# A sliding-window attention with a two-layer network behind it: a batch's last 64-query block and the next batch's first block are scored together

## The chip, the cores and the metric

The kernel runs on one core of one Trainium2 chip. A core has a TensorE (PE in the profile) for matmuls, a VectorE (DVE), a ScalarE (ACT), a GpSimd (POOL) and a SyncE (SP); the last two are used here to issue DMAs, and GpSimd for one iota. PE reads its stationary operand with a separate weight load (PEld). The metric is the device time of one execution in microseconds; the figure that counts is the median of several runs.

## The reference

Attention over 8 batches of 8 heads, 576 positions and 64 features a head, with a linear position bias and a causal window of 128; then a network of two matmuls with a squared ReLU between them, over all 4608 tokens.

```python
scores = np.matmul(q, k.transpose(0, 1, 3, 2)) / sqrt(64)
rel = pos[:, None] - pos[None, :]
mask = (rel >= 0) & (rel < 128)
scores = np.where(mask, scores - slopes[h] * abs(rel), -1e9)   # slopes[h] = 2 ** -(h + 1), 8 heads
attn = softmax(scores) @ v                                     # [8, 8, 576, 64]
x = attn.transpose(0, 2, 1, 3).reshape(4608, 512)
out = np.maximum(x @ w_in, 0) ** 2 @ w_out                     # w_in 512 x 2048, w_out 2048 x 512
```

## The kernel before

**Blocks.** A batch's 576 positions are cut into five blocks, four of 128 and a last one of 64 (`blk`); there are 40 blocks `m`, and `m % 5` is the place in the batch. As the window is 128 wide, a block's queries see the keys of their own block (part 1) and of the one before (part 0); the first block of a batch has part 1 alone. `attention(m)` (L294) does for one block:

- *turn*: K and Q of the block (tile `kq`, loaded by POOL at L276) are transposed into `kqT`. Blocks 0 to 9 do it by eight PE transposes into a PSUM tile `tp` (L317), copied out by DVE (L290) and ACT (L292); from block 10 on by one DMA transpose on SP's queue (`turn_kq`).
- *burst* (L347): the score matmuls of all eight heads, scores transposed (keys on partitions, queries on columns). A head has 64 features, so each matmul uses 64 of the 128 rows of the array, and two heads (`half` 0 and 1) follow each other on the two halves. A middle block has 16 of 128 columns; the last block of a batch 16 of 64 columns; the first block 8 of 128 columns. They go into four PSUM banks of tag `a`.
- *exp* (L360, ACT): four instructions, one a bank, of 512 elements a partition for a middle block and 256 for a last or first block, into a tile `P`.
- *mask* (L368, DVE): four multiplications of `P` by `masks`, which hold exp of the bias inside the window and 0 outside.
- *pv* (L383): P times V for each head and part, with a column of ones in V that sums the weights; then reciprocal (L404) and normalization (L409) on DVE for each half of the heads, into a tile `x`.
- *x turned*: into `xT`, by four PE transposes `xp` (L428) and a copy for blocks 0 to 12, by a DMA transpose on SP for later ones.

**The network.** Tokens go in nine groups of 512. `fc_step` (L461) makes one 128-wide slice of the hidden layer with four 128x512 matmuls into `h`, ACT takes the ReLU (L470), DVE the square (L476). `t_part` (L490) makes a quarter of the 16 matmuls of one 128-token output tile `o`, which ACT copies out (L501) and SP stores.

**Who sets the order.** Nothing is left to a scheduler on the chip: every step is a `Task` with an engine (or a choice of two), a key (its due time), what it depends on, and the `Slot`s of the rings it takes and gives back. `Plan.order()` plays the tasks through with assumed costs and gives each engine its list; the tasks are then emitted in that order, and each engine works through its list in order. So a change of the tasks rearranges all engines, POOL's loads and SP's queue too. The attention of later blocks is laid between the h and o matmuls of earlier groups. Group 0 needs blocks 0 to 3 of batch 0, group 1 blocks 4 to 8. Rings: four PSUM banks `a` (a burst takes all four), two each for `h` and `o`; four `kq`, four `kqT`, six `vt`, three `P`, three `x`.

Of the kernel before, what the change touches and what calls it, by code (L numbers as in the profile page):

```python
# [141 lines left out]
def kernel(  # L142
# [26 lines left out]

    ident = const.tile([128, 128], BF16)  # L170
    masks = const.tile([128, H, 2, 128], BF16)
    dist = const.tile([128, 2, 128], FP32)
    far = const.tile([128, 2, 128], FP32)
    w_in_sb = const.tile([128, C, d_ff], BF16)
# [5 lines left out]

    size = {"kq": 4, "v": 6, "kqT": 4, "P": 3, "x": 3}
    kq = ring("kq", size["kq"], [128, 2, d_model])
    vt = ring("vt", size["v"], [128, H, D + 1])
    kqT = ring("kqT", size["kqT"], [128, 2 * C, 128])
# [41 lines left out]
    for h in range(H):  # L228
        def build_mask(h=h):
            nc.scalar.activation(masks[:, place(h)], dist, AF.Exp, bias=0.0,  # L230
                                 scale=-(2.0 ** (-8.0 * (h + 1) / H)))
        t_mask.append(plan.add({"ACT": act(256)}, -9e5 + h, build_mask, [t_dist]))

    def ones():
        for t in vt:
# [55 lines left out]
        else:  # L291
            nc.scalar.activation(o, i, AF.Copy)  # L292

    def attention(m):  # L294
        b, kb = divmod(m, NKB)
        n = blk[kb]
        due = (b * S + kb * 128 + n) / 4 - 192 - 40
        first = b == 0
        kq_by_dma = m >= KQ_DMA
        x_by_dma = m >= X_DMA  # L300


        sk = sk_of[m] = Slot("kqT")
        both = {"ACT": act(C * n), "DVE": dve(C * n, 2)}
# [25 lines left out]
        t_kq_of[m] = t_kq  # L330


        sP = Slot("P")
        t_P = []
        parts = ([(0, m - 1)] if kb else []) + [(1, m)]
        p0 = parts[0][0]
        slot_s = [Slot("a") for _ in range(4)]

        def burst():

            for sl in slot_s:
                sl.tile = psum.tile([128, 512], FP32, tag="a", bufs=4, name="ps_s")
            for c in range(C):
                for part, mk in parts:
                    for half in range(2):
                        rows = slice(half * 64, half * 64 + 64)
                        nc.tensor.matmul(  # L347
                            slot_s[2 * (c // 2) + half].tile.rearrange("p (c t q) -> p c t q", c=2, t=2)[
                                :, c % 2, part, 0:n],
                            kqT[sk_of[mk].idx][rows, c, :], kqT[sk.idx][rows, C + c, 0:n], start=True, stop=True)  # L350
        rel = [sk_of[mk] for part, mk in parts if part == 0 or kb == NKB - 1]
        tm = plan.add({"PE": 220.0 + C * len(parts) * (max(n, 64) / 2.4 + 4)}, due - 28, burst,
                      [t for _, mk in parts for t in t_kq_of[mk]] + chain["s"], slot_s + [sP], rel)
        chain["s"] = [tm]
        for i in range(4):
            def view(t):
                return t[:, :, p0:2, 0:n]

            def expo(i=i):
                nc.scalar.activation(view(Pt[sP.idx][:, 2 * i:2 * i + 2]),  # L360
                                     view(slot_s[i].tile.rearrange("p (c t q) -> p c t q", c=2, t=2)),
                                     AF.Exp, bias=0.0, scale=scale)
            cols = 2 * n * len(parts)
            te = plan.add({"ACT": act(cols)}, due - 28 + 3 * i, expo, [tm], [], [slot_s[i]])

            def mask(i=i):
                pt = view(Pt[sP.idx][:, 2 * i:2 * i + 2])
                nc.vector.tensor_tensor(pt, pt, view(masks[:, 2 * i:2 * i + 2]), op=ALU.mult)  # L368
            t_P.append(plan.add({"DVE": dve(cols, 2)}, due - 28 + 3 * i, mask, [te] + t_mask))


        sx = Slot("x")
        t_norm = []
        for hf in range(2):
            slot_v = Slot("o" if first else "a")
            last = None
            for hi in range(4):
                h = 4 * hf + hi
                for part, mk in parts:
                    def emit(h=h, hi=hi, part=part, mk=mk, slot_v=slot_v):  # L380
                        if hi == 0 and part == p0:
                            slot_v.tile = psum.tile([128, 512], FP32, tag=slot_v.tag, bufs=plan.bufs[slot_v.tag], name="pv")
                        nc.tensor.matmul(  # L383
                            slot_v.tile[:, hi * (D + 1):(hi + 1) * (D + 1)],
                            Pt[sP.idx][:, place(h), part, :], vt[s_in[mk, "v"].idx][:, h, :],
                            start=part == p0, stop=part == 1)
                    rel = []
                    if hf == 1 and hi == 3:
                        if part == 0 or kb == NKB - 1:
                            rel.append(s_in[mk, "v"])  # L390
                        if part == 1:
                            rel.append(sP)
                    new = hi == 0 and part == p0
                    last = plan.add({"PE": mm(D + 1)}, due - 12 + 4 * hf, emit,
                                    [last, t_P[place(h) // 2], t_in[mk, "v"]]
                                    + (t_P[2 * hf:2 * hf + 2] + chain["pv"] if new else []),
                                    ([slot_v] + ([sx] if hf == 0 else [])) if new else [], rel)
# [37 lines left out]
                     slot_x.tile[:, 0:512].rearrange("p (c t) -> p c t", c=C)[:, :, 0:n])  # L435
            t_xT[b, kb] = plan.add(both if first else {"DVE": both["DVE"]}, due, evac, [last], [], [slot_x])

    sk_of, t_kq_of = {}, {}
    for m in range(NBLK):
        attention(m)  # L440


    def tokens(lo, hi):
# [116 lines left out]
```

The softmax here doesn't subtract the row's maximum and nothing guards it: scores larger than these inputs give would overflow.

## Time and profile before

| | |
|---|---|
| median of 5 runs | 321.72 us (321.22 to 323.79) |
| the profiled execution | 321.04 us |
| its span, first to last instruction | 319.3 us |
| PE busy | 304.2 us, 95% of the span, 2436 matmuls |
| DVE busy, ACT busy, POOL busy | 169.3 us, 178.5 us, 107.4 us |
| granted TensorE clock | 1.000 |
| chain that ended last, by engine | PE 92%, DVE 3%, the rest 1% or less each |

The page gives busy time as the union of an engine's instructions, and "idle before" as the time an engine stood still ahead of a group, with what released it. A matmul's own duration (379 ns for 512 columns) contains a latency that overlaps the next one; how long it holds PE is read from the distance between starts (0.216 us). In the timeline, a row is a run of like instructions: start, length, engine, line, operation, output and inputs, shape, and how many; in brackets the idle time before it and what ended it.

### The profile page before, as it was taken

How to read it: one execution, taken by the hardware profiler on the slowest of the kernel's cores; microseconds unless marked ns; L12 is line 12 of the kernel's file. 1: busy time of each engine (PE TensorE's matmuls, PEld its weight loads, DVE VectorE, ACT ScalarE, POOL GpSimd, SP SyncE). 2: the span in 40 equal slices, each digit the busy share in tenths (PEclk: the TensorE clock that was granted, in tenths of full speed). 3: DMA queues.
4: the chain of work that ended last, by engine and by line, in shares of the span. 5: the costliest groups of instructions: out<-in, count | busy, mean ns of one | idle time of the engine just before them, and what ended most of it. 6: DMA issues, size and time to landing. Idle time of an engine off the chain costs nothing.

```text
span 319.3 us, 6418 instructions
## 1 busy us (share of the span) xinstructions
PE 304.2 (95%) x2436; PEld 154.1 (48%) x2436; DVE 169.3 (53%) x501; ACT 178.5 (56%) x358; POOL 107.4 (34%) x133
## 2 busy tenths in 40 slices
PE   1789989999999999999999999999999999999995
PEld 1565555545545554444444454444444454444442
DVE  4686766566677664555545565555555563222200
ACT  4574765467656755555655554555655563444311
POOL 8975865283255534323433233232100000000000
PEclk9999999999999999999999999999999999999999
DMA  9999999999999999999999999998923111000121
GB/s 67 145 190 176 166 202 162 183 196 112 161 136 151 201 156 164 142 132 117 137 189 107 117 118 141 170 133 115 146 55 84 50 51 41 35 33 33 43 91 66
DMA packets 166783, 39.22 MB, mean 123 GB/s; under 512 B 158048, under 2 KB 162144, under 8 KB 166752
## 3 DMA queue, kind: packets, MB, share of 16 engines
q0 software_dynamic: 116736, 18.36, 83.2%
q1 hardware_dynamic: 50016, 20.46, 33.1%
q8 instruction: 19, 0.31, 0.4%
q14 instruction: 12, 0.10, 0.1%
HBM read 36.70 MB, written 9.44 MB: 145 GB/s over the span
## 4 chain that ended last, share of the span: by engine, by line
PE 92%; DVE 3%; DMA 1%; POOL 1%; ACT 1%; issue 1%; POOLq 0%; ACTq 0%
PE o L490 40%; PE h L461 39%; PE ps_s L347 6%; PE pv L383 5%; PE tp L317 1%; DMA kq<-in_q_dram 1%; PE xp L428 1%; DVE P L368 1%; ACT kqT L292 1%; POOL kq L276 1%; DVE kqT L290 1%; DVE x L409 1%; POOL vt L276 0%; DVE g L476 0%; DVE xT L290 0%
## 5 line engine op out<-in xcount | busy, mean ns | idle before, releaser
L490 PE MATMUL o<-w_out_sb,g 128*128 128x512 bf16 x576 | 149.0, 379 | 0.0
L461 PE MATMUL h<-xT,w_in_sb 128*128 128x512 bf16 x576 | 146.7, 379 | 0.0
L470 ACT ACTIVATE rt<-h 128x512 bf16<-128x512 f32 x144 | 85.8, 603 | 95.0 <-PE h L461 93.5
L476 DVE TENSOR_TENSOR g<-rt 128x512 bf16<-128x512 bf16 x144 | 60.5, 420 | 83.5 <-ACT rt L470 82.6
L461 PEld LDWEIGHTS <-w_in_sb 128*128 128x128 bf16 x576 | 53.6, 98 | 58.1
L490 PEld LDWEIGHTS <-g 128*128 128x128 bf16 x576 | 51.6, 98 | 53.9
L360 ACT ACTIVATE P<-ps_s 128x512 bf16<-128x512 f32 (+1 forms) x160 | 70.2, 519 | 11.2 <-PE ps_s L347 10.9
L368 DVE TENSOR_TENSOR P<-P,masks 128x512 bf16<-128x512 bf16 (+1 forms) x160 | 57.5, 371 | 17.8 <-ACT P L360 13.6
L276 POOL DMA_DIRECT2D kq<-in_k_dram x40 | 34.1, 852 | 77.3 <-DMA kqT<-kq 71.8
L276 POOL DMA_DIRECT2D vt<-in_v_dram x40 | 34.1, 853 | 39.4 <-PE pv L383 35.0
L383 PEld LDWEIGHTS <-P 128*128 128x128 bf16 x576 | 28.5, 99 | 17.8 <-DVE P L368 1.3
L276 POOL DMA_DIRECT2D kq<-in_q_dram x40 | 34.1, 853 | 3.4 <-PE h L461 1.7
L409 DVE TENSOR_TENSOR x<-pv,rec 128x256 bf16<-128x256 f32 (+1 forms) x80 | 33.4, 420 | 1.8
L501 ACT ACTIVATE osb<-o 128x512 f32<-128x512 f32 x36 | 21.7, 602 | 22.2 <-PE o L490 22.2
L383 PE MATMUL pv<-vt,P 128*128 128x65 bf16 x576 | 32.3, 196 | 0.3
L347 PEld LDWEIGHTS <-kqT 64*128 64x128 bf16 x576 | 16.0, 97 | 17.3 <-issue 15.3
L404 DVE RECIPROCAL rec<-pv 128x4 f32<-128x4 f32 (+1 forms) x80 | 14.3, 179 | 19.0 <-PE pv L383 16.7
L347 PE MATMUL ps_s<-kqT 64*128 64x128 bf16 (+1 forms) x320 | 20.5, 218 | 0.9 <-DVE kqT L290 0.8
L347 PE MATMUL ps_s<-kqT,kqT 64*128 64x128 bf16 (+1 forms) x256 | 17.3, 217 | 1.2 <-ACT kqT L292 1.2
L317 PE MATMUL tp<-ident,kq 128*128 128x128 bf16 x80 | 8.5, 261 | 6.6 <-DMA kq<-in_k_dram 5.4
L317 PEld LDWEIGHTS <-kq 128*128 128x128 bf16 x80 | 6.6, 118 | 8.6 <-DMA kq<-in_k_dram 5.7
L428 PE MATMUL xp<-ident,x 128*128 128x128 bf16 x52 | 6.1, 234 | 2.2 <-DVE x L409 2.2
(20 smaller groups left out, 32.1 us busy)
## 6 DMA issues: line engine op xcount, KB each, us to landing
out_dram<-osb SPq DMA_DIRECT2D x36, 256.0 KB, 2.8
kq<-in_k_dram POOLq DMA_DIRECT2D x32, 128.0 KB, 4.6
kq<-in_q_dram POOLq DMA_DIRECT2D x32, 128.0 KB, 5.3
vt<-in_v_dram POOLq DMA_DIRECT2D x32, 128.0 KB, 5.5
w_in_sb<-in_moe_w_in_dram POOLq DMA_DIRECT2D x4, 512.0 KB, 9.6
w_out_sb<-in_moe_w_out_dram POOLq DMA_DIRECT2D x4, 512.0 KB, 9.4
kq<-in_k_dram POOLq DMA_DIRECT2D x8, 64.0 KB, 4.6
kq<-in_q_dram POOLq DMA_DIRECT2D x8, 64.0 KB, 4.8
```

Source lines behind the costliest of these rows:

```text
L276: nc.gpsimd.dma_start(o, src[b, :, kb * 128:kb * 128 + n, :].rearrange("h s d -> s h d"))
L317: nc.tensor.transpose(slot.tile[:, i * 128:(i + 1) * 128], kq[s_in[m, "k"].idx][:, i // C, (i % C) * 128:(i % C + 1) * 128], ident)
L347: nc.tensor.matmul(slot_s[2 * (c // 2) + half].tile.rearrange("p (c t q) -> p c t q", c=2, t=2)[:, c % 2, part, 0:n], kqT[sk_of[mk].idx][r ...
L360: nc.scalar.activation(view(Pt[sP.idx][:, 2 * i:2 * i + 2]), view(slot_s[i].tile.rearrange("p (c t q) -> p c t q", c=2, t=2)), AF.Exp, bia ...
L368: nc.vector.tensor_tensor(pt, pt, view(masks[:, 2 * i:2 * i + 2]), op=ALU.mult)
L383: nc.tensor.matmul(slot_v.tile[:, hi * (D + 1):(hi + 1) * (D + 1)], Pt[sP.idx][:, place(h), part, :], vt[s_in[mk, "v"].idx][:, h, :], star ...
L409: nc.vector.tensor_tensor(xt[sx.idx][0:n, hf * 256:(hf + 1) * 256].rearrange("p (h e) -> p h e", h=4), pv[0:n, :, 0:D], srec.tile[0:n, :]. ...
L461: nc.tensor.matmul(slot.tile[:, 0:w], w_in_sb[:, cc, fc * 128:(fc + 1) * 128], xT[:, cc, g * 512 + lo:g * 512 + hi], start=cc == 0, stop=c ...
L470: nc.scalar.activation(srt.tile[:, 0:w], slot.tile[:, 0:w], AF.Relu, bias=0.0, scale=1.0)
L476: nc.vector.tensor_tensor(sg.tile[:, fc, lo:hi], srt.tile[:, 0:w], srt.tile[:, 0:w], op=ALU.mult)
L490: nc.tensor.matmul(slot.tile, sg.tile[:, fc, t * 128:(t + 1) * 128], w_out_sb[:, fc, :], start=fc == 0, stop=fc == FCB - 1)
L501: nc.scalar.activation(so.tile, slot.tile, AF.Copy)
```

## The change

`attention(m)` is split in three: `turn(m)`, `score(ms)` and `mix(m)`. `score` takes one block, or the last block of a batch with the first of the next one. Of a pair, the last block's two parts lie in columns 0 to 63 and 64 to 127 of a head's 256, and the first block's single part in 128 to 255, so four exps of 512 elements and four masks of 512 serve both. A table `pair_masks` in that layout is made once, by two DVE copies out of `masks`. A third DVE instruction writes zeros into the part of one `kqT` tile that the last block's keys don't fill. The ring `kqT` gets a fifth tile. A pair's burst waits for the keys and queries of both blocks and has the due time of the first. Seven pairs are made; block 0 and block 39 stay alone in theirs.

```diff
--- before.py
+++ after.py
@@ -169,6 +169,7 @@
 
     ident = const.tile([128, 128], BF16)
     masks = const.tile([128, H, 2, 128], BF16)
+    pair_masks = const.tile([128, H, 256], BF16)
     dist = const.tile([128, 2, 128], FP32)
     far = const.tile([128, 2, 128], FP32)
     w_in_sb = const.tile([128, C, d_ff], BF16)
@@ -180,7 +181,7 @@
 
 
 
-    size = {"kq": 4, "v": 6, "kqT": 4, "P": 3, "x": 3}
+    size = {"kq": 4, "v": 6, "kqT": 5, "P": 3, "x": 3}
     kq = ring("kq", size["kq"], [128, 2, d_model])
     vt = ring("vt", size["v"], [128, H, D + 1])
     kqT = ring("kqT", size["kqT"], [128, 2 * C, 128])
@@ -230,6 +231,13 @@
             nc.scalar.activation(masks[:, place(h)], dist, AF.Exp, bias=0.0,
                                  scale=-(2.0 ** (-8.0 * (h + 1) / H)))
         t_mask.append(plan.add({"ACT": act(256)}, -9e5 + h, build_mask, [t_dist]))
+
+    def build_pair():
+        nc.vector.tensor_copy(pair_masks[:, :, 0:128].rearrange("p h (t s) -> p h t s", t=2), masks[:, :, :, 0:64])
+        nc.vector.tensor_copy(pair_masks[:, :, 128:256], masks[:, :, 1, :])
+        nc.vector.memset(kqT[NKB - 1][:, 0:C, 64:128], 0.0)
+
+    t_pair = plan.add({"DVE": 1300.0}, -9e5 + 9, build_pair, t_mask)
 
     def ones():
         for t in vt:
@@ -291,14 +299,15 @@
         else:
             nc.scalar.activation(o, i, AF.Copy)
 
-    def attention(m):
+    def where(m):
         b, kb = divmod(m, NKB)
-        n = blk[kb]
-        due = (b * S + kb * 128 + n) / 4 - 192 - 40
-        first = b == 0
+        return b, kb, blk[kb], (b * S + kb * 128 + blk[kb]) / 4 - 192 - 40, b == 0
+
+    def turn(m):
+        if m in t_kq_of:
+            return
+        b, kb, n, due, first = where(m)
         kq_by_dma = m >= KQ_DMA
-        x_by_dma = m >= X_DMA
-
 
         sk = sk_of[m] = Slot("kqT")
         both = {"ACT": act(C * n), "DVE": dve(C * n, 2)}
@@ -330,45 +339,72 @@
         t_kq_of[m] = t_kq
 
 
+    def score(ms):
+        due = where(ms[0])[3]
         sP = Slot("P")
         t_P = []
-        parts = ([(0, m - 1)] if kb else []) + [(1, m)]
-        p0 = parts[0][0]
+        pair = len(ms) == 2
         slot_s = [Slot("a") for _ in range(4)]
+        work_of = []
+        for i, m in enumerate(ms):
+            b, kb, n, _, first = where(m)
+            parts_of[m] = ([(0, m - 1)] if kb else []) + [(1, m)]
+            P_of[m] = (sP, t_P)
+            for part, mk in parts_of[m]:
+                at = 128 * i + 64 * part if pair and i == 0 else 128 * part
+                at_of[m, part] = at
+                rel = [sk_of[mk]] if part == 0 or kb == NKB - 1 else []
+                work_of.append((m, mk, n, at, rel))
+        lo = min(w[3] for w in work_of)
+        hi = max(w[3] + w[2] for w in work_of)
+        n = 128 if pair else work_of[0][2]
 
         def burst():
 
             for sl in slot_s:
                 sl.tile = psum.tile([128, 512], FP32, tag="a", bufs=4, name="ps_s")
             for c in range(C):
-                for part, mk in parts:
+                for m, mk, w, at, _ in work_of:
                     for half in range(2):
                         rows = slice(half * 64, half * 64 + 64)
                         nc.tensor.matmul(
-                            slot_s[2 * (c // 2) + half].tile.rearrange("p (c t q) -> p c t q", c=2, t=2)[
-                                :, c % 2, part, 0:n],
-                            kqT[sk_of[mk].idx][rows, c, :], kqT[sk.idx][rows, C + c, 0:n], start=True, stop=True)
-        rel = [sk_of[mk] for part, mk in parts if part == 0 or kb == NKB - 1]
-        tm = plan.add({"PE": 220.0 + C * len(parts) * (max(n, 64) / 2.4 + 4)}, due - 28, burst,
-                      [t for _, mk in parts for t in t_kq_of[mk]] + chain["s"], slot_s + [sP], rel)
+                            slot_s[2 * (c // 2) + half].tile.rearrange("p (c x) -> p c x", c=2)[
+                                :, c % 2, at:at + w],
+                            kqT[sk_of[mk].idx][rows, c, :], kqT[sk_of[m].idx][rows, C + c, 0:w],
+                            start=True, stop=True)
+        tm = plan.add({"PE": 220.0 + C * sum(max(w[2], 64) / 2.4 + 4 for w in work_of)}, due - 28, burst,
+                      [t for w in work_of for x in w[:2] for t in t_kq_of[x]] + chain["s"], slot_s + [sP],
+                      [x for w in work_of for x in w[4]])
         chain["s"] = [tm]
         for i in range(4):
             def view(t):
-                return t[:, :, p0:2, 0:n]
+                if pair:
+                    return t
+                return t.rearrange("p c (t q) -> p c t q", t=2)[:, :, lo // 128:2, 0:n]
+
+            def Pv(i=i):
+                return view(Pt[sP.idx][:, 2 * i:2 * i + 2].rearrange("p h t q -> p h (t q)"))
 
             def expo(i=i):
-                nc.scalar.activation(view(Pt[sP.idx][:, 2 * i:2 * i + 2]),
-                                     view(slot_s[i].tile.rearrange("p (c t q) -> p c t q", c=2, t=2)),
+                nc.scalar.activation(Pv(i), view(slot_s[i].tile.rearrange("p (c x) -> p c x", c=2)),
                                      AF.Exp, bias=0.0, scale=scale)
-            cols = 2 * n * len(parts)
+            cols = 2 * sum(w[2] for w in work_of)
             te = plan.add({"ACT": act(cols)}, due - 28 + 3 * i, expo, [tm], [], [slot_s[i]])
 
             def mask(i=i):
-                pt = view(Pt[sP.idx][:, 2 * i:2 * i + 2])
-                nc.vector.tensor_tensor(pt, pt, view(masks[:, 2 * i:2 * i + 2]), op=ALU.mult)
-            t_P.append(plan.add({"DVE": dve(cols, 2)}, due - 28 + 3 * i, mask, [te] + t_mask))
-
-
+                pt = Pv(i)
+                mk = (pair_masks if pair else masks.rearrange("p h t q -> p h (t q)"))[:, 2 * i:2 * i + 2]
+                nc.vector.tensor_tensor(pt, pt, view(mk), op=ALU.mult)
+            t_P.append(plan.add({"DVE": dve(cols, 2)}, due - 28 + 3 * i, mask,
+                                [te] + (([t_pair] if pair else t_mask))))
+
+    def mix(m):
+        b, kb, n, due, first = where(m)
+        x_by_dma = m >= X_DMA
+        parts = parts_of[m]
+        p0 = parts[0][0]
+        sP, t_P = P_of[m]
+        both = {"ACT": act(C * n), "DVE": dve(C * n, 2)}
         sx = Slot("x")
         t_norm = []
         for hf in range(2):
@@ -382,7 +418,9 @@
                             slot_v.tile = psum.tile([128, 512], FP32, tag=slot_v.tag, bufs=plan.bufs[slot_v.tag], name="pv")
                         nc.tensor.matmul(
                             slot_v.tile[:, hi * (D + 1):(hi + 1) * (D + 1)],
-                            Pt[sP.idx][:, place(h), part, :], vt[s_in[mk, "v"].idx][:, h, :],
+                            Pt[sP.idx][:, place(h)].rearrange("p t q -> p (t q)")[
+                                :, at_of[m, part]:at_of[m, part] + 128],
+                            vt[s_in[mk, "v"].idx][:, h, :],
                             start=part == p0, stop=part == 1)
                     rel = []
                     if hf == 1 and hi == 3:
@@ -435,9 +473,16 @@
                      slot_x.tile[:, 0:512].rearrange("p (c t) -> p c t", c=C)[:, :, 0:n])
             t_xT[b, kb] = plan.add(both if first else {"DVE": both["DVE"]}, due, evac, [last], [], [slot_x])
 
-    sk_of, t_kq_of = {}, {}
-    for m in range(NBLK):
-        attention(m)
+    sk_of, t_kq_of, parts_of, P_of, at_of = {}, {}, {}, {}, {}
+    m = 0
+    while m < NBLK:
+        ms = [m, m + 1] if m % NKB == NKB - 1 and m + 1 < NBLK else [m]
+        for x in ms:
+            turn(x)
+        score(ms)
+        for x in ms:
+            mix(x)
+        m += len(ms)
 
 
     def tokens(lo, hi):
```

## Prediction, made before the changed kernel ran

> **What bounds the kernel now.** I read the page's busy shares and slices first, then the waits of TensorE, then TensorE's timeline around one burst of each kind, and last VectorE and TensorE where the largest stall lies.
>
> ```profile
> span 319.3 us, 6418 instructions
> PE 304.2 (95%) x2436; PEld 154.1 (48%) x2436; DVE 169.3 (53%) x501; ACT 178.5 (56%) x358; POOL 107.4 (34%) x133
> PE   1789989999999999999999999999999999999995
> ```
>
> PE is full from slice 9 to the last; DVE and ACT are a little over half busy. So 28 fewer exps and 28 fewer masks are worth nothing by themselves: only what shortens PE's own stream, or removes one of its few stalls, moves the end. PE's waits name the stalls:
>
> ```profile
> PE tp L317 <- DMA kq<-in_k_dram: 5.4, 2, 4.8
> PE xp L428 <- DVE x L409: 2.2, 5, 0.9
> PE ps_s L347 <- ACT kqT L292: 1.2, 2, 0.7
> ```
>
> The columns are total, times, longest. The first is the first load. The second is the largest one that a different order could remove. All others lie before 21 us.
>
> What a burst costs PE is read from where the matmuls around it start (an h or o matmul starts every 0.216 us when nothing intervenes: four fill 0.86):
>
> ```profile
> 223.82 0.59 PE L490 MATMUL o<-w_out_sb,g 128*128 128x512 bf16 x2
> 224.35 0.20 PE L347 MATMUL ps_s<-kqT,kqT 64*128 64x64 bf16 x2
> ...
> 224.57 0.19 PE L347 MATMUL ps_s<-kqT 64*128 64x64 bf16 x2
> 224.69 0.60 PE L490 MATMUL o<-w_out_sb,g 128*128 128x512 bf16 x2
> ...
> 229.07 1.03 PE L461 MATMUL h<-xT,w_in_sb 128*128 128x512 bf16 x4
> 230.03 0.40 PE L347 MATMUL ps_s<-kqT 64*128 64x128 bf16 x8
> 230.36 0.82 PE L490 MATMUL o<-w_out_sb,g 128*128 128x512 bf16 x3
> ```
>
> The two o matmuls before the 64-query burst are through at 223.82 + 2 x 0.216 = 224.25 and the next o starts at 224.69: the burst takes 0.44 us. Its eight pairs start about 0.03 apart (224.35 to 224.57 is seven steps), so 0.24 is work and 0.20 is entering and leaving the half-array matmuls. The first-block burst takes 230.36 - (229.07 + 0.86) = 0.43: four pairs at 0.055 (from the spacing in a sixteen-matmul burst, 209.55 to 209.95 in seven steps) are 0.22, and again 0.21 is the change-over.
>
> **The change, part by part.** Sums are made on the span of 319.3 us. The profiled execution itself took 321.04 us, 1.7 us more than its span, and lies 0.7 us under the median of 321.72; I carry the difference in span over to the median. 0.5% is 1.6 us, about what a measurement here can tell from no change.
>
> (1) *Change-overs.* Seven pairs are made (batches 0 to 6 each end in one); the number of matmuls stays 2436. A merged burst should take 0.24 + 0.22 + 0.20 = 0.66 us where two took 0.87: 0.21 us less. For six of them, in the stretch where PE is full, 6 x 0.21 = 1.26 us comes off the path. The mixed pace, 64 columns and 128 in turn, is in no row. Its ends: 0.03 per narrow pair as in the pure burst, or 0.055 as for wide ones, which adds 8 x 0.025 = 0.20 per burst and takes the whole gain. I take the first, because the narrow matmuls themselves are the same ones.
>
> (2) *The front.* Block 4 of batch 0 used to be scored (22.35) and multiplied (24.33 to 25.14) before the first h matmul at 25.14. Now it waits for block 5, whose burst stood at 33.16, and PE does that work when it is full. What moves behind the first h: 0.24 of narrow pairs (they join a burst that is paid anyway) and 16 pv at 0.0306 (8 in 0.245, at 205.51) = 0.49, together +0.73. What comes off ahead of it: VectorE's block-4 masks (0.26 at 23.56 and 0.68 at 24.07) stand between block 3's last normalization and its xT copy at 24.68, so that copy and the first h come about 0.2 us earlier. In the new order VectorE also copies both halves of block 2's kqT, in 0.76, where ScalarE's half used to wait for VectorE's (0.42 + 0.60 = 1.02): 0.26 in the chain of blocks. So the first h comes 0.2 to 0.7 earlier; I take 0.4. Net +0.3.
>
> (3) *The new mask table.* Two VectorE copies of 1024 elements and a memset of 256 stand ahead of block 0's masks. They start when ScalarE's eight mask exps end, at 7.9. No SBUF-to-SBUF copy is in the trace. The nearest row is the 128x512 bf16 copy from PSUM: 0.42 us, repeated every 0.34, so 0.68 for 1024. At one element a cycle, as the 256-element normalizations go (every 0.34), it would be 1.3. The memset is half of L238's 0.485. So 1.6 us by the first, 2.9 by the second. Block 0's masks take 1.12, and VectorE's next step, kqT of block 1, cannot start before 10.44, when block 1's second load has come and been turned. 7.9 + 1.6 + 1.1 = 10.6 loses 0.15; the slow end loses 1.4. I take the near row and 0.1, inside the rounding of (2). On POOL's side the issues that run beside block 0's masks take 0.91 to 0.93 against 0.88 to 0.89 just before, so by that row two more VectorE copies cost the queue under 0.1 us.
>
> [...]
>
> (4) *The stall at block 6's transposes.*
>
> ```profile
> 42.99 0.60 PE L383 MATMUL pv<-vt,P 128*128 128x65 bf16 x8
> 43.79 0.29 PE L428 MATMUL xp<-ident,x 128*128 128x128 bf16 x2 [0.19 <-DVE x L409]
> 44.97 0.28 PE L428 MATMUL xp<-ident,x 128*128 128x128 bf16 x2 [0.90 <-DVE x L409]
> 45.09 1.03 PE L490 MATMUL o<-w_out_sb,g 128*128 128x512 bf16 x4
> ```
>
> Here pv, reciprocal, normalization and xp follow each other with nothing between on PE. By the pace, eight pv and four xp take 0.25 + 0.22 = 0.47; they took 45.09 - 42.99 = 2.10, so 1.6 us is lost. In the new order seven h matmuls (1.51 us) stand between this pv and xp, and VectorE has one square less (0.34) between the two normalizations: 1.98 - 0.34 = 1.64 of chain against 0.25 + 1.51 = 1.76 of cover. The stall should go. What is late next is block 7's xp: only two o matmuls (0.43) follow its pv, and the same chain without squares took 50.2 - 49.03 = 1.2, so 1.2 - 0.68 = 0.5 comes back there. With a tenth or so at block 7's burst, 0.6 us stays: net -1.0. Its ends are -1.6 and 0.
>
> (5) *With one answer.* The exps go from 64 narrow and 96 wide to 8 and 124; ScalarE saves 56 x 0.264 - 28 x 0.478 = 1.4 us, VectorE 56 x 0.276 - 28 x 0.332 = 6.2, both hidden behind PE (their idle before relu and square is 93.5 and 82.6 us). A pair's P tile is held for two blocks out of a ring of three; h and o matmuls cover that. The kqT ring grows by one, as a pair holds one tile more. POOL keeps its 128 loads with v loads and w_out in slightly another order, ahead of nothing that PE meets late.
>
> Sum: -1.26 + 0.3 - 1.0 = -1.9 us. From the median: 321.7 - 1.9 = **319.8 us**. With (1) whole, (4) whole and the first h 0.7 earlier it is -1.26 - 1.6 + 0.0 = -2.9: 318.8.
>
> **Rivals.** *The gain is given back.* The mixed bursts run at the wide pace, or the stall of (4) comes back in full at blocks 7 and 8, whose chains now start after extra work for block 4 (2 reciprocals, 2 normalizations of 0.31, a copy of 0.2: 1 us of VectorE). For it: neither is in a row. Against: VectorE is 55 to 75% busy there. With (1) at nothing and 0.6 more lost: +0.3 - 1.0 + 0.6 = -0.1, 321.6; with only one of them, 320.5 to 321.
>
> *A pair waits for its second block (slower).* The pair of blocks 9 and 10 is the first whose second block is turned by DMA, and PE is held at its burst until kqT 10 has landed; h matmuls are queued behind it.
>
> ```profile
> 54.49 0.37 SPq L509 DMA_DIRECT2D out_dram<-osb  x1
> 55.05 1.58 SPq L307 DMA_TRANSPOSE kqT<-kq  x1
> ...
> 65.98 0.40 PE L347 MATMUL ps_s<-kqT 64*128 64x128 bf16 x8
> ```
>
> That transpose sits behind the first output store on SP and landed at 63.8, so block 10's burst had 2.2 us to spare, the least of all (later pairs would have over 6). In the new order 37 h matmuls (8.0 us) come ahead of the pair, which puts it near 65 and leaves about 1. From there each microsecond of lateness is one of PE: to be slower by 1.6 it must land 1 + 1.9 + 1.6 = 4.5 us later, at 68.3, giving 323.3. Against: the store's and the transpose's order on SP is unchanged, and transposes issued in that stretch took 5.1 to 8.7 us, this one already 8.7.
>
> *More gain.* All of (4) goes and the front is at its early end: 318.8 or below.
>
> **How the numbers follow.** Forecast 0.56 (own range 318.8 to 320.8), gain given back 0.27, slower 0.10, more gain 0.07. Faster by over 0.5% means below 320.1: all of "more gain", and nine tenths of the forecast: 0.57. The rest of the forecast and the given-back case are within 0.5%: 0.33. Slower 0.10. The range runs from 318.4, a little past the early bounds, to 322.2, where (1) and (4) give nothing and the slow copy takes some tenths.
>
> **What would show it.** Right: wide ps_s bursts of 24 with about 0.66 us between the h and o around them; the first h near 24.7; no xp stall near 43 and half a microsecond at the next xp; ACT x330 and PE full after 60 us. Wrong: a PE wait on a DMA kqT near 65; narrow pairs 0.055 apart; block 1's burst later than 11.55 by half a microsecond, from the copies; or a first h no earlier than 25.1.

## The result, and the profile after

The changed kernel takes 320.64 us (median of 54 runs, 318.27 to 322.31), the kernel before 321.58 us beside it (94 runs, 320.13 to 326.93): ratio 0.9966, 95% interval 0.9955 to 0.9977. That is 0.3% faster, inside the range of the prediction and 0.8 us above its figure. The ratios, here and below, leave out runs that took over 1.5% longer than the fastest of their kernel. The profiled execution took 321.46 us, its span is 319.7 us: it lies 0.8 us above the median, and it shows why.

The page, the lines that answer to those shown of before, with the row of the granted clock added:

```profile
span 319.7 us, 6368 instructions
PE 304.0 (95%) x2436; PEld 153.4 (48%) x2436; DVE 166.9 (52%) x476; ACT 176.1 (55%) x330; POOL 107.5 (34%) x133
PE   1779999999999999999999999999999999999995
PEclk9996999999999999999999999999999999999999
```

ACT has 28 instructions fewer, DVE 25 fewer, PE as many as before. New is the 6 in the clock row: in the slice from 24 to 32 us TensorE had 0.6 of its speed. In the row of before every slice is 9:

```profile
PEclk9999999999999999999999999999999999999999
```

TensorE's timeline of the changed kernel there (start, length, then the group; in brackets the idle time before it):

```profile
23.43 0.40 PE L466 MATMUL xp<-ident,x 128*128 128x128 bf16 x2 [0.18 <-DVE x L447]
24.34 8.86 PE L506 MATMUL h<-xT,w_in_sb 128*128 128x512 bf16 x29 [0.52 <-DVE xT L298]
33.03 0.61 PE L326 MATMUL tp<-ident,kq 128*128 128x128 bf16 x8
```

The 29 h matmuls take 33.03 - 24.34 = 8.69 us where 29 x 0.216 = 6.26 are due: 2.4 us lost with TensorE busy throughout. The same in windows of 3.4 us (length, then busy us and instructions of PE, PEld, DVE, ACT, POOL, then granted clock, DMA share, GB/s):

```profile
19.00:22.40 3.40, 2.29 (x42) 1.46 (x43) 3.33 (x13) 2.39 (x5) 3.21 (x4) 1.00 1.24 205
22.40:25.80 3.40, 2.54 (x14) 1.04 (x14) 1.36 (x4) 0.00 (x0) 0.97 (x2) 0.51 1.24 207
25.80:29.20 3.40, 3.40 (x9) 1.18 (x8) 0.85 (x2) 1.19 (x2) 0.88 (x1) 0.50 1.90 174
29.20:32.60 3.40, 3.40 (x16) 1.47 (x15) 1.28 (x3) 2.24 (x4) 3.35 (x4) 0.99 2.43 155
```

TensorE ran at half speed for two windows, after one in which it was busy 2.29 of 3.4 us. And the kernel before:

```profile
19.00:22.40 3.40, 2.62 (x48) 1.90 (x48) 3.17 (x12) 2.39 (x5) 2.92 (x4) 1.00 1.23 203
22.40:25.80 3.40, 2.79 (x49) 1.77 (x49) 3.33 (x15) 1.21 (x4) 1.15 (x2) 1.00 1.25 208
25.80:29.20 3.40, 3.40 (x20) 1.68 (x19) 1.69 (x5) 1.97 (x4) 0.88 (x1) 1.00 1.90 175
```

Each run lists its mean granted clock, so the share of runs with a fall can be counted. In the profiled runs a fall lasts 3.41 us (e6 and f4, below) or 6.83 (the changed kernel). Over a run of 319 us 3.4 us at half speed make the mean 1 - 1.7/319 = 0.995, 6.8 make 0.989. I count a run as fallen below 0.9965. Where in a run the clock fell is seen only in a profiled run, and three of those show a fall: the changed kernel, e6 and f4, all between 22 and 30 us. A mean of 0.997 can come from the end alone: in the profile of f1 the clock is at half speed from 315.6 us on, after the last matmul, which costs nothing. By my estimate from these numbers a mean of 0.992 would then be a fall of 3.4 us and such an end.

| runs | mean clock | time, median |
|---|---|---|
| changed, 9 of 54 | 0.997 and more | 319.37 us |
| changed, 29 of 54 | 0.992 to 0.995 | 320.64 us |
| changed, 16 of 54 | 0.988 to 0.989 | 321.58 us |
| before, 62 of 87 (the runs beside the experiments) | 0.998 and more | 321.24 us |
| before, 25 of 87 | 0.993 to 0.995 | 323.13 us |

At full clock the changed kernel is 1.9 us faster. But its clock falls in 45 of 54 runs, that of before in 25 of 87, and a fall costs 1.3 to 2.2 us. That is where about half of the gain went: 0.9 us is left between the medians of all runs. (The runs of before in the table were made beside the experiments, not beside the changed kernel.)

The rows of the other terms, all of the changed kernel. The shared burst of blocks 9 and 10, on TensorE's timeline:

```profile
66.58 1.24 PE L506 MATMUL h<-xT,w_in_sb 128*128 128x512 bf16 x5
67.75 0.20 PE L370 MATMUL ps_s<-kqT,kqT 64*128 64x64 bf16 x2
67.79 0.25 PE L370 MATMUL ps_s<-kqT 64*128 64x64 bf16 x4
...
68.14 0.25 PE L370 MATMUL ps_s<-kqT 64*128 64x64 bf16 x4
68.32 0.82 PE L506 MATMUL h<-xT,w_in_sb 128*128 128x512 bf16 x3
```

The five h are through at 66.58 + 5 x 0.216 = 67.66, the next starts at 68.32: 0.66 us. (The groups mix shapes here: "64x64 x4" holds narrow and wide pairs.) No row before it waits for a DMA.

Block 6's and block 7's transposes:

```profile
43.69 0.49 PE L419 MATMUL pv<-vt,P 128*128 128x65 bf16 x8
44.02 1.68 PE L506 MATMUL h<-xT,w_in_sb 128*128 128x512 bf16 x7
45.53 0.39 PE L466 MATMUL xp<-ident,x 128*128 128x128 bf16 x4
...
51.02 0.28 PE L466 MATMUL xp<-ident,x 128*128 128x128 bf16 x2
51.49 0.29 PE L466 MATMUL xp<-ident,x 128*128 128x128 bf16 x2 [0.20 <-DVE x L447]
51.62 1.03 PE L535 MATMUL o<-w_out_sb,g 128*128 128x512 bf16 x4
```

Seven h stand between the second pv and xp, and xp waits for nothing. At block 7 the four xp take 51.62 - 51.02 = 0.60 instead of 0.22: 0.4 us comes back there.

The second mask table on VectorE, and GpSimd's issues beside it:

```profile
7.94 0.43 DVE L236 COPY pair_masks<-masks 128x1024 bf16<-128x1024 bf16 x1
8.28 0.89 DVE L237 COPY pair_masks<-masks 128x1024 bf16<-128x1024 bf16 x1
9.15 0.17 DVE L238 MEMSET kqT<- 128x128 uint32 x1
9.23 0.82 DVE L397 TENSOR_TENSOR P<-P,masks 128x256 bf16<-128x256 bf16 x4
```

```profile
7.14 0.91 POOL L284 DMA_DIRECT2D kq<-in_k_dram  x1
8.01 0.92 POOL L284 DMA_DIRECT2D kq<-in_q_dram  x1
8.87 0.93 POOL L284 DMA_DIRECT2D vt<-in_v_dram  x1
```

From 7.94 to 9.23 the table takes 1.3 us; the second copy takes more than twice as long as the first. And one wait that was not there before, at the first h of group 3:

```profile
116.01 1.03 PE L535 MATMUL o<-w_out_sb,g 128*128 128x512 bf16 x4
117.39 0.59 PE L506 MATMUL h<-xT,w_in_sb 128*128 128x512 bf16 x2 [0.36 <-DMA xT<-x]
```

It waits for block 17's output, turned by DMA. Before, that DMA was issued at 108.9 and had landed at 114.0, 0.8 us ahead of its h, which stood here:

```profile
114.79 1.03 PE L461 MATMUL h<-xT,w_in_sb 128*128 128x512 bf16 x4
```

Now it is issued at 111.2 and lands at 117.3.

### The profile page after: what moved, and what is told of

Read it like the earlier page. It is cut to its first block, busy times and chain, and to the rows that moved or that the text cites. A ratio compares the mean times of both kernels' runs of the same rounds, so it can differ in the third digit from the quotient of the medians.

```text
span 319.7 us, 6368 instructions
## 1 busy us (share of the span) xinstructions
PE 304.0 (95%) x2436; PEld 153.4 (48%) x2436; DVE 166.9 (52%) x476; ACT 176.1 (55%) x330; POOL 107.5 (34%) x133
## 4 chain that ended last, share of the span: by engine, by line
PE 90%; DMA 3%; DVE 2%; POOL 1%; ACT 1%; issue 1%; POOLq 0%; ACTq 0%
PE h L506 39%; PE o L535 38%; PE ps_s L370 5%; PE pv L419 5%; DMA xT<-x 2%; DMA kq<-in_q_dram 1%; PE tp L326 1%; PE xp L466 1%; POOL kq L284 1%; DVE x L447 1%; DVE P L397 1%; DVE kqT L298 1%; ACT P L389 0%; ACT kqT L300 0%; DVE xT L298 0%
## 5 line engine op out<-in xcount | busy, mean ns | idle before, releaser
L506 PE MATMUL h<-xT,w_in_sb 128*128 128x512 bf16 x576 | 149.1, 384 | 0.9 <-DVE xT L298 0.5
L535 PE MATMUL o<-w_out_sb,g 128*128 128x512 bf16 x576 | 147.2, 379 | 0.0
L535 PEld LDWEIGHTS <-g 128*128 128x128 bf16 x576 | 52.5, 98 | 56.4
L389 ACT ACTIVATE P<-ps_s 128x512 bf16<-128x512 f32 (+1 forms) x132 | 68.2, 592 | 14.0 <-PE ps_s L370 13.9
L397 DVE TENSOR_TENSOR P<-P,masks 128x512 bf16<-128x512 bf16 (+1 forms) x104 | 42.3, 411 | 14.7 <-ACT P L389 10.5
L419 PEld LDWEIGHTS <-P 128*128 128x128 bf16 x576 | 27.8, 99 | 17.6 <-DVE P L397 1.5
L419 PE MATMUL pv<-vt,P 128*128 128x65 bf16 x576 | 31.0, 195 | 0.7 <-DVE P L397 0.3
L370 PE MATMUL ps_s<-kqT 64*128 64x128 bf16 (+1 forms) x320 | 19.3, 217 | 0.8 <-DVE kqT L298 0.8
L370 PE MATMUL ps_s<-kqT,kqT 64*128 64x128 bf16 (+1 forms) x256 | 18.6, 216 | 1.1 <-DVE kqT L298 1.1
L397 DVE TENSOR_TENSOR P<-P,pair_masks 128x512 bf16<-128x512 bf16 x28 | 11.8, 423 | 5.1 <-ACT P L389 3.7
```

Source lines behind the costliest of these rows:

```text
L370: nc.tensor.matmul(slot_s[2 * (c // 2) + half].tile.rearrange("p (c x) -> p c x", c=2)[:, c % 2, at:at + w], kqT[sk_of[mk].idx][rows, c, : ...
L389: nc.scalar.activation(Pv(i), view(slot_s[i].tile.rearrange("p (c x) -> p c x", c=2)), AF.Exp, bias=0.0, scale=scale)
L397: nc.vector.tensor_tensor(pt, pt, view(mk), op=ALU.mult)
L419: nc.tensor.matmul(slot_v.tile[:, hi * (D + 1):(hi + 1) * (D + 1)], Pt[sP.idx][:, place(h)].rearrange("p t q -> p (t q)")[:, at_of[m, part ...
L506: nc.tensor.matmul(slot.tile[:, 0:w], w_in_sb[:, cc, fc * 128:(fc + 1) * 128], xT[:, cc, g * 512 + lo:g * 512 + hi], start=cc == 0, stop=c ...
L535: nc.tensor.matmul(slot.tile, sg.tile[:, fc, t * 128:(t + 1) * 128], w_out_sb[:, fc, :], start=fc == 0, stop=fc == FCB - 1)
```

## Experiments

All medians are in us; ratios are against runs of the kernel before on the same chip. e1 to e4 shared one chip, e5 to e8 another, f1 to f4 a third. Each is the changed kernel with the edit shown, unless said otherwise.

**Which part of the change lowers the clock?** The first reading (A): block 4's scores and pv no longer stand ahead of the first h, and TensorE idles.

e1 leaves batch 0 alone:

```diff
-        ms = [m, m + 1] if m % NKB == NKB - 1 and m + 1 < NBLK else [m]
+        ms = [m, m + 1] if m % NKB == NKB - 1 and NKB <= m and m + 1 < NBLK else [m]
```

> Pairs in batches 1 to 6 only; batch 0's last block and batch 1's first are scored apart, so TensorE does block 4's work ahead of the first h matmul as before. Theory A (what the pairs save is worth about 2 us at full clock, and the granted clock falls to half for some microseconds after the first h because block 4's work no longer fills TensorE between 20 and 24 us): the clock is as in the kernel before, near 1.000; six change-overs of 0.21 us are saved, the stall at block 6's transposes stays: 321.6 - 1.3 = 320.3 us. Theory B (the fall of the clock has nothing to do with the order in front, and the expected gain is missing for another reason, a slower mixed burst or stalls at the pairs): clocks spread as in the changed kernel, 0.988 to 1.000, and a time within 0.3 us of the changed kernel or of the kernel before.

Measured 320.63, ratio 0.9967 (0.9942 to 0.9993). Block 4's work is ahead of the first h again, and still the clock falls in 9 of 12 runs. A alone doesn't hold. The stall at block 6's transposes is back, in TensorE's waits from 30 to 60 us:

```profile
PE xp L466 <- DVE x L447: 1.1, 2, 0.9
```

e2 makes the first pair only:

```diff
-        ms = [m, m + 1] if m % NKB == NKB - 1 and m + 1 < NBLK else [m]
+        ms = [m, m + 1] if m == NKB - 1 else [m]
```

> Only the pair of blocks 4 and 5. Theory A: the front is that of the changed kernel, so most runs show a clock of 0.988 to 0.995; the stall at block 6's transposes is gone (-1.0 us) and the front's work costs +0.3, the clock costs 1 to 2.5 us in most runs: 321.6 + 0.3 to 321.6 + 1, that is 321.9 to 322.6 us. Theory B: clock like the kernel before, 320.9 us.

Measured 321.12, ratio 0.9994 (0.9973 to 1.0015); the clock falls in 10 of 12 runs. In the same stretch of its trace xp waits 0.2 us: e1 and e2 together show that the stall is removed by the pair in batch 0, not by shared bursts as such (in e5 below, also without that pair, xp waits 1.1 us again).

e3 fills the gaps ahead of the first h with matmuls that compute nothing; e4 does it to the kernel before:

```diff
+                        if m == 3 and hi == 0 and part == p0:
+                            for _ in range(3):
+                                nc.tensor.matmul(slot_v.tile[:, 260:508], ident, masks...[:, 0:248], ...)
...
+                if g == 0 and fc == 0 and cc == 0:
+                    for _ in range(3):
+                        nc.tensor.matmul(slot.tile[:, 0:w], ident, masks...[:, 0:512], ...)
```

> The changed kernel with nine matmuls whose results nobody reads, put where TensorE stands still ahead of the first h: three of 248 columns before each half of block 3's pv and three of 512 columns before the first h. They keep TensorE busy for about 1.3 us of the time between 20.5 and 24.3 us. Theory A: the clock stays at 1.000 in nearly all runs and the median falls from 320.6 to 319.2-319.6 us. Theory B: the clocks spread as in the changed kernel and the time is 320.6 us, or up to 0.7 us more.

> The kernel before with the same nine matmuls. Theory A: its own front already keeps the clock up in most runs, so it gains little, 0 to 0.5 us: 321.1 to 321.6 us; some added matmuls may lie on the path and cost 0.2. Theory B (fillers help whatever the order): it gains as much as the changed kernel does.

e3 measured 319.83, ratio 0.9958 (0.9931 to 0.9986); 9 of 12 runs keep 0.997 or more. e4 measured 322.03, ratio 1.0029 (1.0001 to 1.0057); 11 of 12 keep it. Work that costs 0.3% in the kernel before costs nothing in the changed one, and the falls become rare.

**Is it the second mask table?** Theory C: built between the first masks, it lets full clock arrive earlier, so that too little work is left for 19 to 24 us. In the profiles of both kernels TensorE starts at half pace. In the changed kernel the pairs of 128-column score matmuls start 0.107 us apart in the burst at 11.88 us and 0.055 apart in that at 18.92; in the kernel before it is 0.107 in the burst at 15.27 and 0.055 in that at 19.68. (The clock row reads 1.00 before that too, so the pace has to be read from the starts.) The pace doubles near 15.7 us in the changed kernel and near 19.5 in the one before. e5 is e1 with the table built after block 4's output is turned, and its memset moved to the first instructions; e6 is the kernel before with the table added in the early place, read by nothing, and a memset of another tile:

```diff
# e5, against e1 (the move of the memset is not shown)
-    t_pair = plan.add({"DVE": 1300.0}, -9e5 + 9, build_pair, t_mask)
+        if m == NKB:
+            t_pair = plan.add({"DVE": 1300.0}, -9e5 + 9, build_pair, t_mask + [t_xT[0, NKB - 1]])
# e6, against the kernel before
+    t_pair = plan.add({"DVE": 1300.0}, -9e5 + 9, build_pair, t_mask)
```

> The changed kernel with two edits: the burst is shared only at the ends of batches 1 to 6 (block 4 alone again), and the second mask table is built after block 4's turn instead of between the first masks, so that all of the first 23 us is the kernel before. Theory C (the table between the first masks moves copies between VectorE and ScalarE, full clock arrives one step earlier, near 15.6 instead of 18.9 us, TensorE then has too little to do from 19 to 24 us and the clock falls back for some 5 us): full clock arrives at 18.9 to 20.3 us as before, the granted clock is 0.999 or more in about four runs of five, time 319.9 to 320.4 us, that is 1.0 to 1.4 below the kernel before (6 change-overs of 0.21 us, and the stall at block 6 partly back). Rival A (the clock falls whenever block 4's work is missing from the front) falls with e1 and expects the same here. Rival D (the fall comes with the shared bursts or their later order, not with the table): the clock is at 0.992 to 0.995 in most runs as in e1, time near 320.6.

> The kernel before with one addition: the second mask table (two VectorE copies and a small memset) is built at the same place as in the changed kernel, and nothing reads it. Theory C: full clock arrives near 15.6 to 16.4 us instead of 18.9, the first h starts 0.3 to 0.8 us earlier, the granted clock is 0.988 to 0.995 in most runs, and the time is 0 to 1 us above the kernel before (a fall costs 1 to 2 us and the earlier start gives part of it back). Rival D: the table takes 1.3 us of VectorE in the front and moves the first h by -0.3 to +0.7 us; the clock is at 0.999 or more in four runs of five, as before; time within 0.5 us of before.

e5: 321.65, ratio 0.9998 (0.9973 to 1.0024), full clock arrives at 18.1 us, and the clock falls in 7 of 12 runs. e6: 321.20, ratio 0.9965 (0.9931 to 1.0000), falls in 5 of 12, full clock at 18.0. C expected few falls in e5 and many in e6; it got neither. What it did not expect either: with the early table both kernels seem faster.

f3 asks the same with all seven pairs and block 17 turned by TensorE, table late, against f1 with the table early:

```diff
# f3, against f1 (the move of the memset, as in e5, is not shown)
-    t_pair = plan.add({"DVE": 1300.0}, -9e5 + 9, build_pair, t_mask)
+        if m == NKB - 1:
+            t_pair = plan.add({"DVE": 1300.0}, -9e5 + 9, build_pair, t_mask + [t_xT[0, NKB - 2]])
```

> f1's kernel with the second mask table built after block 3's turn, near 21 us, instead of between the first masks; all seven shared bursts stay. Theory C (the early table brings full clock one step earlier and with it the fall): full clock arrives near 18.5 us, the clock stays at 0.997 or more in at least half of the runs, and the time is 0.5 to 1 us below f1's. Theory F without C (block 4's missing work leaves the gap whatever the table does): the clock falls in as many runs as in f1, and the time is within 0.4 us of f1's.

f3: 321.62, ratio 0.9957 (0.9926 to 0.9988). Full clock arrives at 18.8 us, 0.7 before that of the kernel before, and the clock falls in 8 of 12 runs. As the cause C is out. That the early table adds to the falls is not excluded: e1 and e6, with the front of the kernel before and the early table, fall in 14 of 24 runs, the kernel before in 25 of 87.

**Is it the amount of work in that stretch?** Theory F. f1 is the changed kernel with one edit, block 17's output turned by TensorE; f2, f4 and e8 add extra matmuls to it: all nine in another place, at block 6 and group 1 (f2), the last three alone (f4), all nine as in e3 (e8).

```diff
# f1
-        x_by_dma = m >= X_DMA
+        x_by_dma = m >= X_DMA and m != 17
# f2: f1 with e3's matmuls, and
-                        if m == 3 and hi == 0 and part == p0:
+                        if m == 6 and hi == 0 and part == p0:
-                if g == 0 and fc == 0 and cc == 0:
+                if g == 1 and fc == 0 and cc == 0:
# f4: f1 with e3's second group alone (ahead of the first h)
```

> The changed kernel with block 17's output turned by TensorE and no extra matmuls. Against the changed kernel it should gain the 0.36 us wait at group 3's first h less 0.25 us for the four transposes: 0 to 0.4 us. If the nine extra matmuls are what keeps the clock up in e3 and e8 (theory F), the granted clock falls here in most runs as in the changed kernel (0.988 to 0.995) and the time is 320.0 to 321.0; runs that keep full clock should lie 1.5 to 2 us lower, near 318.8. Rival: e8's full clock comes from this edit or from the chip it ran on, and this kernel keeps 0.997 or more in most runs, near 318.8.

> A control for the place of the fill: e8's kernel with the same nine extra matmuls put where TensorE has no gap (six in front of block 6's two halves of pv, three in front of group 1's first h) instead of into the idle stretch ahead of the first h. Theory F (the clock falls because TensorE is idle too much of 19 to 24 us): the clock falls in most runs as in f1, and the time is 0.5 to 1.3 us above f1's (six of 0.1 and three of 0.22 us, partly in gaps). Rival (any nine extra matmuls, or a changed program layout, keep the clock up): 0.997 or more in most runs, 318.7 to 320.

> e8's kernel with a third of the fill: only the three 512-column matmuls ahead of the first h, not the six ahead of block 3's pv. Theory F as a matter of dose (each us of work put into the idle stretch makes a fall rarer): falls in a share of runs between f1's and e8's, a quarter to a half, and a median between theirs, 318.8 to 320. Rival (only the last gap, right ahead of the first h, matters): as e8, all or nearly all runs at 0.997 or more and near 318.8; (only the gaps before it matter): as f1.

f1: 319.42, ratio 0.9914 (0.9881 to 0.9948), 2 of 6 runs fallen. That is fewer than F expects, and closer to its rival: for the first 100 us its order is that of the changed kernel, which falls in 45 of 54; with six runs this stays open. f2, the control: 321.06, ratio 0.9983 (0.9960 to 1.0006), 11 of 12 fallen. (In its profile TensorE also waits 1.6 us for loads of keys and queries near 31 us, so its time is not the price of nine matmuls.) Up to block 6, near 39 us, TensorE's order in e2, f1 and f2 is that of the changed kernel: taken together, 68 of 84 runs with this front fall, and 4 of 30 of e3, e7 (below) and e8, which have the nine matmuls in its gaps. f4: 319.93, ratio 0.9924 (0.9895 to 0.9952), 5 of 6 fallen, three of them with a mean of 0.995, one fall of 3.4 us. Its windows show that three matmuls in the last gap come too late:

```profile
19.00:22.40 3.40, 2.35 (x41) 1.43 (x38) 3.36 (x13) 2.39 (x5) 1.95 (x3) 1.00 1.23 201
22.40:25.80 3.40, 2.77 (x14) 1.35 (x16) 1.54 (x6) 0.00 (x0) 1.71 (x2) 0.53 1.24 205
25.80:29.20 3.40, 3.40 (x16) 1.50 (x15) 1.07 (x3) 1.79 (x3) 0.92 (x2) 0.97 1.75 178
```

The clock is down from 22.6 us to 26.0, and the extra matmuls begin at 23.83. Whether they shorten the fall is not shown: none of the six runs has a mean of 0.989 or less, but of the changed kernel's 45 fallen runs 29 have none either.

**The change-over, and block 17.** e7 is e3 without the sharing itself: each block keeps a burst, exps and masks of its own, and waits as a pair would (the edit of `score` that makes it wait is not shown). e8 is e3 with f1's edit.

```diff
# e7, against e3
-        score(ms)
+        for x in ms:
+            score([x], ms)
```

> The kernel of e3 (changed kernel, with 9 extra matmuls in front of the first h that keep TensorE busy) with one part undone: the narrow and the wide block each keep a burst, an exp tile and masks of their own, though both still wait for the turns of both blocks. The granted clock should be 0.997 or more in most runs, as in e3, so that change-overs are left alone. Theory (term 1 is real: each shared burst saves 0.21 us of TensorE): the time is 1.0 to 1.6 us above e3's 319.83, near 321.1, and bursts of 8 and 16 pairs show 0.44 and 0.43 us each between their last pair and the next matmul. Rival (shared bursts save nothing; the gain of e3 is only the front and the stall at block 6): within 0.3 us of e3.

> The kernel of e3 with one edit: block 17's output is turned by TensorE (four 128x128 transposes in 0.25 to 0.3 us and a VectorE copy) instead of by a DMA. In e3 the first h of group 3 waits 1.69 us for that DMA, in the changed kernel 0.36 us. Theory (the wait is TensorE's own idle time, so all of it but the transposes comes back): time 0.2 to 1.4 us below e3's 319.83, 318.4 to 319.6, and no wait for a DMA at the first h of group 3. Rival (the time is given back at the next change-over, or the turn on TensorE has to wait for VectorE's norm as long as the DMA took): within 0.2 us of e3.

e7: 322.22, ratio 1.0001 (0.9972 to 1.0030), 1 of 12 fallen; 0.43% above e3 by the ratios, 1.4 us, though the intervals overlap a little. The two differ in more than the sharing: at group 3's first h e7 waits 0.4 us where e3 waits 1.7 (below), and ahead of pv e7 waits 0.5 us that e3 doesn't. So the sign is supported, and the size rests on the rows. On TensorE's timeline its narrow burst has h matmuls on both sides:

```profile
63.67 1.03 PE L513 MATMUL h<-xT,w_in_sb 128*128 128x512 bf16 x4
64.63 0.20 PE L370 MATMUL ps_s<-kqT,kqT 64*128 64x64 bf16 x2
...
64.97 1.69 PE L513 MATMUL h<-xT,w_in_sb 128*128 128x512 bf16 x7
...
69.14 1.24 PE L513 MATMUL h<-xT,w_in_sb 128*128 128x512 bf16 x5
70.31 0.40 PE L370 MATMUL ps_s<-kqT 64*128 64x128 bf16 x8
70.64 1.68 PE L513 MATMUL h<-xT,w_in_sb 128*128 128x512 bf16 x7
```

64.97 - (63.67 + 4 x 0.216) = 0.44 and 70.64 - (69.14 + 5 x 0.216) = 0.42, against 0.66 for both in one: 0.2 us a pair, 1.4 for seven by the rows.

e8: 318.71 (318.43 to 318.88), ratio 0.9896 (0.9859 to 0.9934), all 6 runs at 0.998 or more. It has the lowest median of all kernels run and is 1% faster than the kernel before. In e3 the first h of group 3 waits:

```profile
115.69 0.59 PE L512 MATMUL h<-xT,w_in_sb 128*128 128x512 bf16 x2 [1.69 <-DMA xT<-x]
```

In e8 no wait of TensorE for a DMA is left after the first loads, and its windows keep full clock:

```profile
19.00:22.40 3.40, 2.74 (x48) 1.91 (x48) 3.33 (x14) 2.39 (x5) 3.10 (x4) 1.00 1.24 205
22.40:25.80 3.40, 2.89 (x20) 1.43 (x22) 1.35 (x4) 0.52 (x1) 0.88 (x1) 1.00 1.25 208
```

**All kernels side by side**, by the work that TensorE has from 19 to 25.8 us (the sum of those two windows, one profile a kernel, those whose own clock had not fallen there):

| busy of 6.8 us | kernels | runs fallen |
|---|---|---|
| 5.57 to 5.63 | e3, e4, e7, e8 (nine extra matmuls in the gaps) | 5 of 42 |
| 5.41 to 5.43 | before, e1, e5 | 25 of 87, 9 of 12, 7 of 12 |
| 4.59 to 4.66 | e2, f1, f2, f3 | 31 of 42 |

Filling the gaps changes the share, while the same matmuls elsewhere don't. So the work in the stretch ahead of the first h is shown as a cause. It is not the only one: in the middle row the same amount gives very different shares, on the one chip that e1 shared with the kernel before 9 of 12 against 6 of 35.

Nor does TensorE's busy time alone say when the clock falls. In the three profiles with a fall it begins 6.83 us, twice 3.41, after full clock arrived: at 22.47 us after 15.65 in the changed kernel, at 24.84 after 18.01 in e6, at 22.59 after 15.77 in f4; it lasts 6.83, 3.41 and 3.41 us. In the 3.41 us ahead of these falls TensorE was busy 2.30, 2.56 and 2.29 us. Counted in the same way, in steps of 3.41 us from the arrival of full clock, the profiles of e2, f1, f2 and f3 each have a window with 2.07 to 2.16 us of work and no fall after it; that window holds the first h matmuls. f1 also has one ahead of the first h with 2.36 and no fall. Nor do windows at fixed times tell them apart: from 19.0 to 22.4 us TensorE was busy 2.03 us in f2, 2.22 in e2 and 2.31 in f1, all at 1.00 up to 25.8 us. What else decides which run falls was not tried.

## Why the prediction was right or wrong, by its own steps

The measured time lies in the range and 0.8 us above the figure, but what moved it is in none of the terms: the range was drawn without a fall of the clock. That the time came out inside it is partly luck. (The three terms of the sum add to -1.96 us, which the prediction writes as -1.9; the table's 0.1 makes it -1.86.)

**(1) Change-overs: right by the rows.** 0.66 us was expected and measured, and the narrow pairs keep their pace. e7, without the sharing, is 1.4 us slower than e3, but other waits differ between the two as well. The pair of batch 0 took a little longer, about 0.73.

**(2) The front: its rows were nearly right, but the sum lacked a term.** The first h comes at 24.34, 0.8 us earlier (0.4 was taken, 0.7 the end), although most loads ahead of it landed 0.1 to 0.4 later. Full clock also arrived 3.8 us earlier, which is not in the sum; in f3, where it arrived 0.7 earlier, the first h is 0.5 earlier, at 24.60. I counted block 4's work as something to be paid behind the first h and nowhere asked what the emptier stretch does to the clock. That is the term that failed: 2.4 us in the profiled run, 1.3 to 2.2 in most others. All of the sum was made at the clock of the profile of before, 1.00 in every slice, and in 25 of 87 runs of that kernel it is not so either.

By one span, the terms measured are: change-overs -1.26; the front 0.73 - 0.8 = -0.07; block 6's stall -1.6 and 0.4 back, -1.2; group 3's wait +0.36; the clock +2.4. Together +0.2, and the spans differ by +0.4.

**(3) The table: perhaps the wrong sign, and unexplained.** The copies took 0.34 and 0.87 us instead of 0.68 each, and the whole table 1.3 us where 1.6 was expected. The row of block 1's burst, 11.88 instead of 11.55, is explained by its load, which landed 0.33 later. But three comparisons, each at the edge of its intervals, suggest that the early table is worth 0.3 to 0.4% and not +0.1 us: e6 against before (0.9965), e1 against e5 (0.9967 to 0.9998), f1 against f3 (0.9914 to 0.9957). The third is mostly the clock: among runs that keep it, f1 and f3 differ by 0.2 us (4 runs each), while e6 is 1.0 below the kernel before on its chip (7 runs against 19). No row of the traces shows where: the profiled execution of e5 has even a shorter span than that of e1, 317.8 against 318.4 us. At full clock e5 shows no gain at all (321.22 in 5 runs), where six change-overs should give 1.3. So the agreement of -1.9 us at full clock with the sum of -1.9 is partly luck too.

The second copy, which starts 0.27 us into an issue of GpSimd, takes 0.87 us instead of 0.34. GpSimd's issues beside the two stay at 0.91 to 0.93, so it is the copy that takes longer, not the issues. The reason was not tried. (The prediction's slow end, 1.3 us a copy, was an estimate: four times the 0.34 us of a 256-element normalization. How many cycles an element takes is in no row.)

**(4) The stall at block 6: right.** It went whole, 0.4 instead of 0.5 came back at block 7, and e1 brings it back by undoing batch 0's pair. What I didn't follow is the next thing down the stream, block 17's DMA turn, which had 0.8 us to spare at group 3's first h. In the changed kernel it is issued 2.3 us later and the h waits 0.36; in e3 it is issued 0.7 earlier but takes 7.4 us instead of 5.1, the h is due 0.8 sooner, and it waits 1.69.

**(5) Hidden work: right as far as the rows go.** ACT runs 28 and DVE 25 instructions fewer, their busy time falls by 2.4 us each (1.4 was expected of ACT, and of DVE 6.2 less the table), and TensorE is as full after 60 us as before. No run has this change alone.

**The rivals.** The slower one did not happen: kqT 10 landed at 62.8, the pair's burst came at 67.75. The gain was in part given back, and the median of 320.64 lies where that rival put it with one of its two mechanisms, 320.5 to 321; but neither is the reason: bursts run at the narrow pace and the stall stayed away.

**Pauses.** The longest pause of TensorE between 17 and 25 us is 0.56 us in the profile of the changed kernel, where the clock fell, and 0.63 in that of the kernel before, where it did not. So the longest pause does not tell the two apart. Nor does the busy time of 3.41 us: three falls came after 2.3 to 2.6 us of work, and no fall came after windows with as little as 2.1.

## What to carry to other kernels

Before taking work out of a stretch where the busiest engine already has gaps, ask what the clock of TensorE does there: count the mean clock of all runs, not only that of one profile. Moving work behind a late start can cost more than the work: here 0.73 us were moved, and the profiled run lost 2.4 us to the clock. A few matmuls that compute nothing, put into the gaps, can give it back: with nine of them 3 of 12 runs fell (e3) where 45 of 54 fell without; put elsewhere (f2) 11 of 12 fell, and with three in the last gap alone (f4) 5 of 6. When a stall goes, look for the next transfer whose lead it has shortened; here four transposes in place of one DMA settled it (group 3's first h waits 1.69 us in e3 and not at all in e8).

## What the runs showed of the hardware

- In three profiles (the changed kernel, e6, f4) the granted clock halved after 3.41 us in which TensorE was busy 2.3 to 2.6 us; in the changed kernel with no pause over 0.56 us between 17 us and the fall. The fall began 6.8 us after full clock had arrived, and it lasted 3.41 or 6.83 us. By their mean clocks it came in some runs and not in others of the same kernel (45 of 54, 25 of 87 before). Which run falls was not explained.
- Two equal copies of 128x1024 bf16 in SBUF, one after the other, held VectorE for 0.34 and 0.87 us.
- Alternating pairs of 64-column and 128-column matmuls on half the array kept the pace of each: two narrow pairs and a wide one start again after 0.12 us, where 2 x 0.03 + 0.055 = 0.115 are due, and a burst of 24 took 0.66 us, with one change-over.
